# Long convolution by a two-stage FFT with soft-MoE slots: z loads of a pair of chunks in 16 KB rows, issued in the step before, with five z store buffers

## The chip, the cores and the metric

The kernel runs on one core of one Trainium2 chip. The metric is the device time of a run in microseconds. Before the change it is 991.8 us in the median of 11 runs (981.59 to 1000.34).

## The reference, cut to what matters

```
x (8, 5696, 128), h (5696, 128):  y = irfft(rfft(x, 2S) * rfft(h, 2S))[:, :S]      # causal long convolution, per channel
t = y.reshape(45568, 128)
logits = t @ phi                         # phi (128, 32): 8 experts x 4 slots
d = softmax of logits over the tokens    # per slot
slot_input = d.T @ t                     # (32, 128)
slot_out[e] = relu(slot_input[e] @ w1[e]) @ w2[e]     # w1 (8, 128, 1024), w2 (8, 1024, 128)
c = softmax of logits over the slots     # per token
out = c @ slot_out                       # (45568, 128)
```

All data is float32.

## The kernel before

The convolution is a transform of length 90 x 64 in two stages and its inverse in two stages, written as matrix products. The filter h is run through the forward part as group 0, and the 8 batches of x follow as groups 1 to 8. Three kinds of work are interleaved in one loop over `t`, a **step**:

- **A** (`load_x`, `fold`, `stage_a`; steps 0 to 71, eight per group). SP loads a chunk of x (`xc`, three buffers, three steps ahead), GpSimd folds it (L193), TensorE multiplies by `s1` (L204), ScalarE evicts to `fst` (L206, three buffers), and SP stores it to the DRAM tensor `f` (L210, four transfers per step).
- **B** (`load_g`, `stage_b1`, `stage_b2`; from step 9). A group has 23 units, three per step and two in the eighth step. A unit loads `gt` from `f` (L223, five buffers, ordered four units ahead), is transformed (L237, to the PSUM tile `bt`), multiplied by the filter on VectorE (L258, L261, L263), transformed back (L277, to `bz`), evicted by ScalarE to `zst` (L281, **three buffers**) and stored by SP to the DRAM tensor `z` (L282).
- **C** (from step 26). Two chunks are a **pair** T; four pairs (NQ) make a batch. A pair's z (two chunks, two loads of 90 rows x 8 KB, L307) comes into the tiles `zc`. `stage_c1` is the last stage of the inverse transform: four products (L329) of two chunks each, with an eviction to `y` by ScalarE (L338), sums on VectorE (L334, L335) and GpSimd (L348). `stage_c2` to `stage_c6` transpose, form logits and both softmaxes, and add to the slots (L357, L366, L395, L418, L442, L466). A pair takes two steps: c1 is in the even one, c2 and c3 in the odd one.

The order of instructions on each engine is the order in which the program writes them (`tc.manual_schedule()`). Almost all transfers go through SP's queue in that order. They take eight semaphores in rotation, so that a transfer waits for the one that SP issued eight places before, and everything behind it on SP waits too. The banks of PSUM go round in a ring of four; the fourth product of c1 uses the bank that the first one left, so it waits for the eviction by L338.

In a step, the body of the loop has this order: tables, **`load_pair`** (before the change), `load_x`, `stage_a(t, 0)`, dispatch, `slot_b()`, `stage_c1` with `stage_c4` between its products, c2, c6, `slot_b()`, the GpSimd part of c1, c5, `stage_a(t, 1)`, c3, `slot_b()`. A `slot_b()` issues the `gt` load of a unit four ahead, the first half of one unit and the second half (with the z store) of the one before it. The load of a pair is issued at the start of the odd step ahead of its c1:

```
        if pair(1 - 2 * ahead) is not None:
            load_pair(pair(1 - 2 * ahead))
```

`pair(lag)` gives T where the step is `26 + lag + 2 T`. `ahead` is 1 until the last B unit is done (step 81); then memory is free, further z tiles (`zd`) are added to the ring `zring`, and loads are issued a pair earlier. The first load of a batch reads what the last B units of that batch stored, so it has to wait for those stores.

A z load has 90 rows, in partitions 20 to 109 (`Z0 = 20`); a row is 8 KB long in `z`, and rows follow at 64 KB there. The table `i1`, by which c1 multiplies, has its rows in the same partitions, and zeros in the others; the zc tiles are zeroed once in full (L296).

Of the kernel before, what the change touches and what calls it, by code (L numbers as in the profile page):

```python
# [10 lines left out]
F32 = mybir.dt.float32  # L11
# [3 lines left out]
PSUM = bass.MemoryType.PSUM  # L15


def transform_tables(S, N1, N2, CH, Z0, X0, F0, F1):

    N, R1, HALF, P = N1 * N2, S // N2, N2 // 2, 2 * N2
    k1 = np.arange(N1)
    alpha = np.pi * (k1 + 0.5) / N1
    m1 = np.arange(R1) - (N1 - 1) / 2
    a1 = np.outer(m1, alpha)
    s1 = np.stack([np.cos(a1), -np.sin(a1), -np.cos(a1)], 1)
    a0 = np.outer(alpha, np.arange(N1 // 2) + 0.5)
    i1 = np.stack([np.cos(a0), -np.sin(a0), -np.cos(a0)], 1)
    NP = N1 // 2
    part = s1  # L40
    s1 = np.zeros((P, 3, P))
    for a, p in enumerate((F0, F1)):
        s1[X0:X0 + R1, :, p:p + NP] = part[:, :, a * NP:(a + 1) * NP]
    i1 = np.pad(i1[np.arange(N1).reshape(2, N1 // 2).T.reshape(-1)],
                [(Z0, P - N1 - Z0), (0, 0), (0, N2 - N1 // 2)])
    k2 = np.arange(N2)
    omega = np.pi * (k1[:, None] + 2 * N1 * k2[None] + 0.5) / N
    m2 = np.arange(HALF) - (N2 - 1) / 2
    a2 = m2[None, :, None] * omega[:, None, :]
    w = np.concatenate([np.cos(a2), np.sin(a2)], 1)  # L50
    back = np.arange(N2).reshape(2, HALF // CH, CH).transpose(1, 0, 2).reshape(-1)
    NU = (NP + 1) // 2
    turn = (N1 - 1) / 2 * alpha[:, None] + (N2 - 1) / 2 * omega
    wq = np.zeros((2, N2, NP, N2))
    vq = np.zeros((2, N2, NU, 2, N2))
    tn = np.zeros((2, N2, 2, NU, 2))
    for a in range(2):
        wq[a] = w[a * NP:(a + 1) * NP].transpose(1, 0, 2)
        for q in range(NP):
            vq[q % 2, :, q // 2, a] = w[a * NP + q][back].T  # L60
            tn[q % 2, :, 0, q // 2, a] = np.cos(turn[a * NP + q]) / N
            tn[q % 2, :, 1, q // 2, a] = np.sin(turn[a * NP + q]) / N
    wq, vq, tn = [t.reshape(P, *t.shape[2:]) for t in (wq, vq, tn)]
    return [np.ascontiguousarray(t, dtype=np.float32) for t in (s1, i1, wq, vq, tn)]
# [3 lines left out]
def kernel(  # L68
# [24 lines left out]
    nc = tc.nc  # L93
    P = 128
# [14 lines left out]
    NQ = NJ // 2  # L109
    assert S == R1 * N2 and R1 == N1 - 1 and D == P and CH == Q == 4  # L110
    SPLIT = R1 // 16 * 16
    Z0, X0, F0, F1 = 20, 20, 6, 82
    ctx.enter_context(tc.manual_schedule())

    t_s1, t_i1, t_w, t_v, t_turn = [
        nc.inline_tensor(t, f"tab_{n}").ap()
        for n, t in zip(("s1", "i1", "w", "v", "turn"), transform_tables(S, N1, N2, CH, Z0, X0, F0, F1))]
    fd = [nc.dram_tensor(f"f_{g}", (2, N2, NP, 2, D), F32, kind="Internal").ap() for g in range(B + 1)]
    zd = [nc.dram_tensor(f"z_{b}", (NP, 2 * N2, 2, D), F32, kind="Internal").ap() for b in range(B)]
    cd = nc.dram_tensor("c_t", (P, B * NQ, Q, 2, MH), F32, kind="Internal").ap()  # L120
# [50 lines left out]
    def load_x(c):  # L171
        if c >= (B + 1) * NJ:
            return
        g, j = divmod(c, NJ)
        src = (h if g == 0 else x[g - 1]).rearrange("(a n) d -> a n d", n=N2)
        t_ = xcs[c % len(xcs)]
        gap = N2 - CH * (2 * j + 1)
        for r in (slice(0, SPLIT), slice(SPLIT, R1)):
            v = src[r, CH * j:CH * (j + 1), :]
            v = bass.AP(tensor=v.tensor, offset=v.offset,  # L180
                        ap=[v.ap[0], [gap * D, 2], [1, CH * D]])
            nc.sync.dma_start(
                out=t_[X0 + r.start:X0 + r.stop, :, :, :].rearrange("p s n d -> p s (n d)"), in_=v)
        xs[c] = t_
# [82 lines left out]
    def stage_b2(u):  # L267
        g, i = divmod(u, NU)
        if g == 0:
            return  # L270
        n = min(2, NP - 2 * i)
        y_ = prods.pop(u)
        bz = bps.tile([P, 2, 512], F32, name="bz", tag="bz")
        for q in range(n):
            r = slice(q * HP, (q + 1) * HP)
            for a in range(2):
                nc.tensor.matmul(bz[a * HP:(a + 1) * HP, q, 0:2 * D], vt[r, i, a, :],  # L277
                                 y_[r, a, :, :].rearrange("p c d -> p (c d)"),
                                 start=True, stop=True)
        st = bpool.tile([P, 2, 2 * D], F32, name="zst", tag="zst", bufs=3)  # L280
        nc.scalar.activation(st[:, 0:n, :], bz[:, 0:n, 0:2 * D], AF.Copy)  # L281
        nc.sync.dma_start(  # L282
            out=zd[g - 1][2 * i:2 * i + n, :, :, :].rearrange("q r c d -> r q (c d)"),
            in_=st[:, 0:n, :])
# [2 lines left out]

    zs, ys, Ls, ds = {}, {}, {}, {}
    ybufs = [ypool.tile([P, Q * CH, D + 1], F32, name=f"y{i}") for i in range(2)]
    zring = [ypool.tile([P, 2, CH, 2, D], F32, name=f"zc{i}") for i in range(2)]  # L290
    lt = ypool.tile([P, CH, 2, HP], F32, name="lt")
    dt = ypool.tile([P, CH, 2, HP], F32, name="dt")
    om, op = [ypool.tile([P, CH, D], F32, name=n) for n in ("om", "op")]
    yt = ypool.tile([D, Q * CH, 2, MH], F32, name="yt")
    for t_ in zring:
        nc.vector.memset(t_[:, :, :, :, :], 0.0)  # L296
    for t_ in (lt, dt):
        nc.vector.memset(t_[:, :, :, :], 0.0)
    for t_ in ybufs:
        nc.vector.memset(t_[:, :, D:D + 1], 1.0)  # L300

    def load_z(c):
        b, j = divmod(c, NJ)
        t_ = zring.pop(0)
        zring.append(t_)
        w_ = 2 * CH * 2 * D
        nc.sync.dma_start(  # L307
            out=t_[Z0:Z0 + N1, :, :, :, :].rearrange("k o n c d -> k (o n c d)"),
            in_=zd[b].rearrange("q (a r) c d -> (q a) (r c d)",
                                a=2)[:, j * w_:(j + 1) * w_])  # L310
        zs[c] = t_

    def load_pair(T):
        if T < NT:
            load_z(2 * T)
            load_z(2 * T + 1)

    def stage_c1(T, between):
        za, zb = zs.pop(2 * T), zs.pop(2 * T + 1)
        y_ = ybufs[T % 2]  # L320

        def part(v, f):
            k = (2 * v + f) * CH
            return y_[:, k:k + CH, 0:D] if f == 0 else y_[:, k + CH - 1:k - 1:-1, 0:D]

        def product(o, tab, q):
            p = bank()
            for h_, t_ in enumerate((za, zb)):
                nc.tensor.matmul(p[h_ * HP:(h_ + 1) * HP, :], i1[:, tab, :], t_[:, o, :, q, :],  # L329
                                 start=True, stop=True)  # L330
            return p[:, :].rearrange("p (n d) -> p n d", d=D)

        def fold_out(even, minus, plus):
            nc.vector.tensor_tensor(out=plus, in0=even, in1=minus, op=AL.add)  # L334
            nc.vector.tensor_tensor(out=minus, in0=even, in1=minus, op=AL.subtract)  # L335

        b_, a_ = product(0, 1, 1), product(0, 0, 0)
        nc.scalar.activation(part(0, 0), b_, AF.Copy)  # L338
        fold_out(a_, part(0, 0), part(1, 0))
        between()  # L340
        b_, a_ = product(1, 1, 0), product(1, 2, 1)
        nc.scalar.activation(om[:, :, :], b_, AF.Copy)

        def after():
            fold_out(a_, om[:, :, :], op[:, :, :])
            for v, o_ in ((1, op), (0, om)):
                for part_, sign in ((part(v, 1), AL.subtract), (part(v, 0), AL.add)):
                    nc.gpsimd.tensor_tensor(out=part_, in0=part(v, 0), in1=o_[:, :, :], op=sign)  # L348

        ys[T] = y_  # L350
        return after
# [193 lines left out]
    for t in range(steps):  # L545
        us = list(units(t))

        def pair(lag):
            T, half = divmod(t - LAG_C - lag, 2)
            return T if half == 0 and 0 <= T < NT else None  # L550
# [18 lines left out]
        for tab, src, first, n, k in ((wt, t_w, LAG_B - 2, NP, 2 * PER),  # L569
                                      (vt, t_v, LAG_B + NJ - 2, NU, PER)):  # L570
            p0 = k * (t - first)
            if 0 <= p0 < n:
                v = slice(p0, min(n, p0 + k))
                nc.sync.dma_start(out=tab[:, v], in_=src[:, v])
        if pair(1 - 2 * ahead) is not None:
            load_pair(pair(1 - 2 * ahead))
        if t < NA:
            load_x(t + 3)
            stage_a(t, 0)
            fold(t + 1, 0)  # L580
        if pair(3) is not None:
# [11 lines left out]
        if pair(5) is not None:  # L593
            stage_c6(pair(5))
        slot_b()
        if after:
            after()
        if U is not None:
# [21 lines left out]
        if t == last_front:  # L620
            front.close()
            rings.append(mid.enter_context(tc.tile_pool(name="ps2", bufs=4, space=PSUM)))
            last = work.enter_context(tc.tile_pool(name="last", bufs=1))
            tail["last"] = last
            tail["cT"] = last.tile([P, B, R1, 2 * NJ], F32, name="cT")
            tail["pool"] = cload.enter_context(tc.tile_pool(name="cload", bufs=3))
            w2s = last.tile([P, E, NFC, D], F32, name="w2s")
            for i in range(2):
                t_ = last.tile([P, 2, CH, 2, D], F32, name=f"zd{i}")
                nc.vector.memset(t_[:, :, :, :, :], 0.0)  # L630
                zring.insert(i, t_)
            assert pair(1) is not None
            load_pair(pair(1) + 2)
            ahead = 2
# [147 lines left out]
```

## Time and profile before

| | |
|---|---|
| median of 11 runs | 991.8 us (981.59 to 1000.34) |
| the profiled execution | 993.06 us, of which the span from first to last instruction is 991.3 us |
| granted TensorE clock, mean | 0.945 |
| TensorE, VectorE, ScalarE, GpSimd busy | 867.8 us (88%), 675.1 (68%), 510.3 (51%), 462.0 (47%) |
| bytes moved by DMA, mean rate | 272.79 MB, 275 GB/s |
| z loads | 64 transfers of 720 KB (60 to zc, 4 to zd) |
| z stores | 184 transfers, 176 of 256 KB and 8 of 128 KB |
| stages | A alone to about 45 us, A and B to about 190, A, B and C to about 740, B and C to about 830, C alone to about 875, then experts and output |

The page gives busy shares of the engines and the DMA queues over 40 slices of the span. A busy share says how full a resource is; which of the full ones makes the others wait is read from the waits (an engine, its line, what released it, and total, number and longest of such waits), from a tile's view (the same for the instructions of that tile) and from the timeline (single instructions with the idle time ahead of them). In the windows view each row is a stretch of the span with the busy time of PE, PEld, DVE, ACT and POOL, the granted clock, the DMA share and GB/s.

### The profile page before, as it was taken

The numbers are of one execution on the slowest core, as the hardware profiler recorded it, in microseconds if no ns is written. First come the engines' busy times: TensorE is split into PE (matmuls) and PEld (weight loads), VectorE is DVE, ScalarE is ACT, GpSimd is POOL, SyncE is SP. The second block draws the span as 40 slices with busy tenths as digits, with TensorE's granted clock in tenths as the row PEclk, the third lists the DMA queues.
The fourth block names the chain that finished last, engine by engine and source line by source line (L and its number), as shares of the span: only waits on it lengthen the run. The fifth ranks groups of instructions, "written<-read, shape, count | busy, mean of one in ns | idle before, by whom it ended". The sixth has DMA issues, their size and how long they took to land.

```text
span 991.3 us, 20314 instructions
## 1 busy us (share of the span) xinstructions
PE 867.8 (88%) x7220; PEld 406.6 (41%) x7220; DVE 675.1 (68%) x1137; ACT 510.3 (51%) x1051; POOL 462.0 (47%) x427
## 2 busy tenths in 40 slices
PE   6777888799999999999999999999998887785893
PEld 2222233234444444444444444434443343333783
DVE  2034477468888788787878788778877996564542
ACT  3557554345565566556555555556554443442442
POOL 5546533245555555455545555545533442785000
PEclk9989899999999999999999999999999998976875
DMA  7998899899999999999999899999987896942598
GB/s 193 270 276 269 254 330 300 253 314 291 279 289 303 287 285 283 296 291 284 281 301 291 264 300 288 285 268 288 316 262 253 276 290 207 271 174 99 212 405 329
DMA packets 177283, 272.79 MB, mean 275 GB/s; under 512 B 15024, under 2 KB 119728, under 8 KB 171423
## 3 DMA queue, kind: packets, MB, share of 16 engines
q1 hardware_dynamic: 176607, 271.13, 88.3%
q8 instruction: 58, 0.95, 0.4%
q10 hardware_dynamic: 576, 0.36, 0.1%
q14 instruction: 42, 0.34, 0.1%
HBM read 143.04 MB, written 128.39 MB: 274 GB/s over the span
## 4 chain that ended last, share of the span: by engine, by line
PE 51%; DMA 24%; DVE 7%; POOL 6%; ACT 4%; issue 4%; SPq 3%; ACTq 0%; DVEq 0%; POOLq 0%
PE bank L204 16%; DMA z<-zst 11%; PE bank L329 9%; PE bt L237 8%; PE bz L277 6%; DMA zc<-z 5%; POOL y L348 5%; DMA out_dram<-o 4%; PE bank L357 3%; PE bank L442 2%; PE bank L366 2%; DMA f<-fst 1%; SPq L210 1%; DMA gt<-f 1%; DVE yf L263 1%
## 5 line engine op out<-in xcount | busy, mean ns | idle before, releaser
L204 PE MATMUL bank<-x,s 128*128 128x512 f32 x576 | 284.9, 622 | 9.6 <-POOL x L193 7.8
L193 POOL TENSOR_TENSOR x<-xc 128x512 f32<-128x512 f32 x144 | 183.8, 1277 | 144.7 <-PE bank L204 116.2
L281 ACT ACTIVATE zst<-bz 128x512 f32<-128x512 f32 (+1 forms) x184 | 108.2, 588 | 236.1 <-PE bz L277 136.7
L206 ACT ACTIVATE fst<-bank 128x512 f32<-128x512 f32 x288 | 168.3, 597 | 84.8 <-PE bank L204 70.2
L258 DVE TENSOR_TENSOR pr<-bt,Hr 128x512 f32<-128x512 f32 (+1 forms) x184 | 126.6, 688 | 84.6 <-PE bt L237 81.4
L237 PE MATMUL bt<-gt,wt 64*64 64x256 f32 x1620 | 139.4, 408 | 40.0 <-DMA gt<-f 11.4
L263 DVE TENSOR_TENSOR yf<-pr,pi 128x512 f32<-128x512 f32 (+1 forms) x184 | 158.3, 860 | 6.4
L329 PE MATMUL bank<-zc,i 128*64 128x512 f32 x480 | 140.1, 626 | 22.4 <-ACT y L338 15.5
L204 PEld LDWEIGHTS bank<-x,s 128*128 128x128 f32 x576 | 100.4, 193 | 132.5 <-issue 91.6
L277 PE MATMUL bz<-yf,vt 64*64 64x256 f32 x1440 | 119.5, 387 | 7.0 <-DVE yf L263 4.4
L261 DVE TENSOR_TENSOR pi<-bt,Hi 128x512 f32<-128x512 f32 (+1 forms) x184 | 125.2, 681 | 0.0
L237 PEld LDWEIGHTS bt<-gt,wt 64*64 64x64 f32 x1620 | 44.7, 133 | 156.0 <-PE bank L204 54.2
L348 POOL TENSOR_TENSOR y<-y,op 128x512 f32<-128x512 f32 x64 | 75.7, 1184 | 59.1 <-DVE op L334 56.6
L403 POOL MEMSET dt<- 64x8 f32 x32 | 3.4, 107 | 180.8 <-ACT dn L406 121.8
L348 POOL TENSOR_TENSOR y<-y,om 128x512 f32<-128x512 f32 x64 | 85.2, 1331 | 2.5
L357 PE MATMUL bank<-ident,y 109*128 109x109 f32 x512 | 62.4, 270 | 12.7 <-POOL y L348 12.6
L277 PEld LDWEIGHTS bz<-yf,vt 64*64 64x64 f32 x1440 | 53.7, 134 | 46.0 <-issue 9.4
L329 PEld LDWEIGHTS bank<-zc,i 128*64 128x64 f32 x480 | 33.7, 138 | 93.2 <-issue 37.5
L359 ACT ACTIVATE yt<-bank 128x360 f32<-128x360 f32 x128 | 53.0, 471 | 30.4 <-PE bank L357 30.4
L248 DVE SCALAR_TENSOR_TENSOR Hr<-bt,turn,ph 128x128 f32<-128x128 f32 (+1 forms) x46 | 16.1, 349 | 74.8 <-ACT ph L246 74.8
L357 PEld LDWEIGHTS bank<-ident,y 109*128 109x128 f32 x512 | 50.4, 145 | 29.3 <-POOL y L348 20.8
L334 DVE TENSOR_TENSOR y<-bank,y 128x512 f32<-128x512 f32 x32 | 22.1, 691 | 51.2 <-ACT y L338 45.8
(95 smaller groups left out, 915.9 us busy)
## 6 DMA issues: line engine op xcount, KB each, us to landing
f<-fst SPq DMA_DIRECT2D x288, 180.0 KB
gt<-f SPq DMA_DIRECT2D x198, 256.0 KB
z<-zst SPq DMA_DIRECT2D x176, 256.0 KB
zc<-z SPq DMA_DIRECT2D x60, 720.0 KB
xc<-in_x_dram SPq DMA_DIRECT2D x64, 320.0 KB
out_dram<-o SPq DMA_DIRECT2D x16, 1024.0 KB
out_dram<-o SPq DMA_DIRECT2D x8, 768.0 KB
c_t<-cst SPq DMA_DIRECT2D x26, 180.0 KB
```

The source lines that it names most:

```text
L193: nc.gpsimd.tensor_tensor(out=y_[:, :, :], in0=t_[:, 0, :, :], in1=t_[:, 1, ::-1, :], op=AL.subtract if comp else AL.add)
L204: nc.tensor.matmul(p[:, :], s1[:, tab[G], :], src[:, :, :].rearrange("p n d -> p (n d)"), start=True, stop=True)
L206: nc.scalar.activation(st[:, :, G, :], p[:, :].rearrange("p (n d) -> p n d", d=D), AF.Copy)
L237: nc.tensor.matmul(bt[q * HP:(q + 1) * HP, a, 0:2 * D], wt[r, 2 * i + q, :], t_[r, q, :, :].rearrange("p c d -> p (c d)"), start=True, sto ...
L258: nc.vector.tensor_tensor(out=pr[r, :, :, :], in0=pv, in1=Hr[r, i, :, :].unsqueeze(2).broadcast_to([n * HP, 2, 2, D]), op=AL.mult)
L261: nc.vector.tensor_tensor(out=pi[r, :, :, :], in0=pv, in1=Hi[r, i, :, :, :], op=AL.mult)
L263: nc.vector.tensor_tensor(out=y_[r, :, :, :], in0=pr[r, :, :, :], in1=pi[r, :, ::-1, :], op=AL.add)
L277: nc.tensor.matmul(bz[a * HP:(a + 1) * HP, q, 0:2 * D], vt[r, i, a, :], y_[r, a, :, :].rearrange("p c d -> p (c d)"), start=True, stop=True)
L281: nc.scalar.activation(st[:, 0:n, :], bz[:, 0:n, 0:2 * D], AF.Copy)
L329: nc.tensor.matmul(p[h_ * HP:(h_ + 1) * HP, :], i1[:, tab, :], t_[:, o, :, q, :], start=True, stop=True)
L348: nc.gpsimd.tensor_tensor(out=part_, in0=part(v, 0), in1=o_[:, :, :], op=sign)
L357: nc.tensor.transpose(p[:, i * TR:(i + 1) * TR], ys[T][0:TR, k * CH + i, 0:D], ident[0:TR, 0:TR])
```

## The change

The two z loads of a pair (one per chunk, 90 rows of 8 KB) become two loads that hold both chunks (64 rows and 26 rows, each of 16 KB). The 64 rows go to partitions 32 to 95 and the other 26 to partitions 0 to 25, and the rows of `i1` follow them. The two zc tiles become one tile of the same total size. The load of a pair that isn't the first of its batch is issued in the even step, after the second `slot_b()`, which is the step in which the pair before it is read for the last time. The load of a batch's first pair stays at the start of the odd step, now behind `load_x`. With `ahead` at 2 the same places hold, one pair earlier. The z store tile `zst` has five buffers instead of three.

```diff
...
 PSUM = bass.MemoryType.PSUM
-def transform_tables(S, N1, N2, CH, Z0, X0, F0, F1):
+def z_blocks(n):
+
+    return [(0, 64, 32), (64, n - 64, 0)]
+
+
+def transform_tables(S, N1, N2, CH, X0, F0, F1):
...
     s1 = np.zeros((P, 3, P))
     for a, p in enumerate((F0, F1)):
         s1[X0:X0 + R1, :, p:p + NP] = part[:, :, a * NP:(a + 1) * NP]
-    i1 = np.pad(i1[np.arange(N1).reshape(2, N1 // 2).T.reshape(-1)],
-                [(Z0, P - N1 - Z0), (0, 0), (0, N2 - N1 // 2)])
+    part = i1[np.arange(N1).reshape(2, NP).T.reshape(-1)]
+    i1 = np.zeros((P, 3, N2))
+    for r, n, p in z_blocks(N1):
+        i1[p:p + n, :, 0:NP] = part[r:r + n]
     k2 = np.arange(N2)
     omega = np.pi * (k1[:, None] + 2 * N1 * k2[None] + 0.5) / N
     m2 = np.arange(HALF) - (N2 - 1) / 2
...
     NQ = NJ // 2
     assert S == R1 * N2 and R1 == N1 - 1 and D == P and CH == Q == 4
     SPLIT = R1 // 16 * 16
-    Z0, X0, F0, F1 = 20, 20, 6, 82
+    X0, F0, F1 = 20, 6, 82
     ctx.enter_context(tc.manual_schedule())
     t_s1, t_i1, t_w, t_v, t_turn = [
         nc.inline_tensor(t, f"tab_{n}").ap()
-        for n, t in zip(("s1", "i1", "w", "v", "turn"), transform_tables(S, N1, N2, CH, Z0, X0, F0, F1))]
+        for n, t in zip(("s1", "i1", "w", "v", "turn"), transform_tables(S, N1, N2, CH, X0, F0, F1))]
     fd = [nc.dram_tensor(f"f_{g}", (2, N2, NP, 2, D), F32, kind="Internal").ap() for g in range(B + 1)]
     zd = [nc.dram_tensor(f"z_{b}", (NP, 2 * N2, 2, D), F32, kind="Internal").ap() for b in range(B)]
     cd = nc.dram_tensor("c_t", (P, B * NQ, Q, 2, MH), F32, kind="Internal").ap()
...
                 nc.tensor.matmul(bz[a * HP:(a + 1) * HP, q, 0:2 * D], vt[r, i, a, :],
                                  y_[r, a, :, :].rearrange("p c d -> p (c d)"),
                                  start=True, stop=True)
-        st = bpool.tile([P, 2, 2 * D], F32, name="zst", tag="zst", bufs=3)
+        st = bpool.tile([P, 2, 2 * D], F32, name="zst", tag="zst", bufs=5)
         nc.scalar.activation(st[:, 0:n, :], bz[:, 0:n, 0:2 * D], AF.Copy)
         nc.sync.dma_start(
             out=zd[g - 1][2 * i:2 * i + n, :, :, :].rearrange("q r c d -> r q (c d)"),
...
     zs, ys, Ls, ds = {}, {}, {}, {}
     ybufs = [ypool.tile([P, Q * CH, D + 1], F32, name=f"y{i}") for i in range(2)]
-    zring = [ypool.tile([P, 2, CH, 2, D], F32, name=f"zc{i}") for i in range(2)]
+    zring = [ypool.tile([P, 2, 2, CH, 2, D], F32, name="zc")]
     lt = ypool.tile([P, CH, 2, HP], F32, name="lt")
     dt = ypool.tile([P, CH, 2, HP], F32, name="dt")
     om, op = [ypool.tile([P, CH, D], F32, name=n) for n in ("om", "op")]
     yt = ypool.tile([D, Q * CH, 2, MH], F32, name="yt")
-    for t_ in zring:
-        nc.vector.memset(t_[:, :, :, :, :], 0.0)
+    nc.vector.memset(zring[0][:, :, :, :, :, :], 0.0)
     for t_ in (lt, dt):
         nc.vector.memset(t_[:, :, :, :], 0.0)
     for t_ in ybufs:
         nc.vector.memset(t_[:, :, D:D + 1], 1.0)
-    def load_z(c):
-        b, j = divmod(c, NJ)
+    def load_pair(T):
+        if T >= NT:
+            return
+        b, j = divmod(T, NQ)
         t_ = zring.pop(0)
         zring.append(t_)
-        w_ = 2 * CH * 2 * D
-        nc.sync.dma_start(
-            out=t_[Z0:Z0 + N1, :, :, :, :].rearrange("k o n c d -> k (o n c d)"),
-            in_=zd[b].rearrange("q (a r) c d -> (q a) (r c d)",
-                                a=2)[:, j * w_:(j + 1) * w_])
-        zs[c] = t_
-
-    def load_pair(T):
-        if T < NT:
-            load_z(2 * T)
-            load_z(2 * T + 1)
+        w_ = 2 * 2 * CH * 2 * D
+        for r, n, p in z_blocks(N1):
+            nc.sync.dma_start(
+                out=t_[p:p + n, :, :, :, :, :].rearrange("k h o n c d -> k (h o n c d)"),
+                in_=zd[b].rearrange("q (a r) c d -> (q a) (r c d)",
+                                    a=2)[r:r + n, j * w_:(j + 1) * w_])
+        zs[T] = t_
     def stage_c1(T, between):
-        za, zb = zs.pop(2 * T), zs.pop(2 * T + 1)
+        t_ = zs.pop(T)
         y_ = ybufs[T % 2]
         def part(v, f):
...
         def product(o, tab, q):
             p = bank()
-            for h_, t_ in enumerate((za, zb)):
-                nc.tensor.matmul(p[h_ * HP:(h_ + 1) * HP, :], i1[:, tab, :], t_[:, o, :, q, :],
-                                 start=True, stop=True)
+            for h_ in range(2):
+                nc.tensor.matmul(p[h_ * HP:(h_ + 1) * HP, :], i1[:, tab, :],
+                                 t_[:, h_, o, :, q, :], start=True, stop=True)
             return p[:, :].rearrange("p (n d) -> p n d", d=D)
         def fold_out(even, minus, plus):
...
             if 0 <= p0 < n:
                 v = slice(p0, min(n, p0 + k))
                 nc.sync.dma_start(out=tab[:, v], in_=src[:, v])
-        if pair(1 - 2 * ahead) is not None:
-            load_pair(pair(1 - 2 * ahead))
         if t < NA:
             load_x(t + 3)
+        V = pair(1 - 2 * ahead)
+        if V is not None and not V % NQ:
+            load_pair(V)
+        if t < NA:
             stage_a(t, 0)
             fold(t + 1, 0)
         if pair(3) is not None:
...
         if pair(5) is not None:
             stage_c6(pair(5))
         slot_b()
+        V = pair(-2 * ahead)
+        if V is not None and V % NQ:
+            load_pair(V)
         if after:
             after()
         if U is not None:
...
             tail["cT"] = last.tile([P, B, R1, 2 * NJ], F32, name="cT")
             tail["pool"] = cload.enter_context(tc.tile_pool(name="cload", bufs=3))
             w2s = last.tile([P, E, NFC, D], F32, name="w2s")
-            for i in range(2):
-                t_ = last.tile([P, 2, CH, 2, D], F32, name=f"zd{i}")
-                nc.vector.memset(t_[:, :, :, :, :], 0.0)
-                zring.insert(i, t_)
+            t_ = last.tile([P, 2, 2, CH, 2, D], F32, name="zd")
+            nc.vector.memset(t_[:, :, :, :, :, :], 0.0)
+            zring.insert(0, t_)
             assert pair(1) is not None
             load_pair(pair(1) + 2)
             ahead = 2
```

## The prediction

> **What bounds the kernel now.** I read the slices of the page first, then the windows around one z load, then the waits of ScalarE and of the SP queue, then the tile view of zc, and last the timeline of one pair. The page's slices (PE, DMA and GB/s; one slice is 24.8 us):
>
> ```profile
> PE   6777888799999999999999999999998887785893
> ...
> DMA  7998899899999999999999899999987896942598
> GB/s 193 270 276 269 254 330 300 253 314 291 279 289 303 287 285 283 296 291 284 281 301 291 264 300 288 285 268 288 316 262 253 276 290 207 271 174 99 212 405 329
> ```
>
> From about 190 to 740 us two resources are full at once: TensorE at 9, the DMA engines at 9. The rate is only 260 to 300 GB/s, though the end of the kernel reaches 405. The windows show why (us; busy time of PE, PEld, DVE, ACT, POOL; clock, DMA share, GB/s):
>
> ```profile
> 533.00:541.00 8.00, 8.00 (x92) 3.95 (x88) 7.83 (x15) 4.88 (x9) 5.47 (x5) 1.00 1.01 334
> 542.00:550.00 8.00, 8.00 (x66) 3.71 (x68) 6.16 (x9) 5.32 (x12) 4.94 (x5) 1.00 0.93 231
> ...
> 565.00:567.00 2.00, 1.85 (x24) 0.90 (x22) 1.86 (x3) 1.20 (x4) 2.00 (x2) 1.00 0.05 17
> ```
>
> The first window holds small stores and loads, 334 GB/s. The second holds one pair's z load, 231 GB/s with the engines as busy: the z load is the slow transfer. In the packet records its 5760 packets of 8 KB last 502 ns in the mean, the shortest 309; 15 engines at 8 KB per 502 ns are 245 GB/s. The third is a hole in the DMA work at a batch boundary. The waits (total us, times, longest), ScalarE first, then SP:
>
> ```profile
> ACT zst L281 <- DMA z<-zst: 93.5, 28, 5.5
> ```
>
> ```profile
> SPq L282 <- DMA zc<-z: 41.8, 14, 4.2
> ...
> SPq L223 <- DMA zc<-z: 35.0, 17, 3.5
> ...
> SPq L307 <- DMA z<-zst: 23.8, 12, 4.4
> ```
>
> ScalarE stands until an old z store has landed and frees one of three buffers; SP stands behind z loads that have not landed, since an SP transfer waits for the one eight places before it (the instruction list names eight semaphores in rotation). What this does to TensorE is in the tile view of zc (idle ahead of the zc matmuls and weight loads, us, times), and in the timeline of one pair (start, length, what, [idle before it <- releaser]):
>
> ```profile
>   ACT y L338: 46.7, 35
> ...
>   DMA zc<-z: 25.8, 29
> ```
>
> ```profile
> 550.82 2.47 PE L329 MATMUL bank<-zc,i 128*64 128x512 f32 x8
> ...
> 554.03 0.60 ACT L281 ACTIVATE zst<-bz 128x512 f32<-128x512 f32 x1 [3.54 <-DMA z<-zst]
> 554.53 0.59 ACT L338 ACTIVATE y<-bank 128x512 f32<-128x512 f32 x1
> ...
> 555.17 1.08 PE L329 MATMUL bank<-zc,i 128*64 128x512 f32 x4 [0.29 <-ACT y L338]
> ```
>
> ScalarE's zst eviction waits 3.54 us for a store, the y eviction behind it is late, and the fourth product of stage c1 waits for the bank that y frees. Taking from the timeline the first zc matmul of each pair, c1 runs 4.4 us undisturbed (from 290.3 and from 362.9) and up to 7.4 (from 336.4 and 407.4); the excess over 4.4 sums to 38 us over pairs 0 to 23. Landing times agree: the pair that starts at 312.6 has its z landed at 312.3, the one at 550.8 at 550.3, the one at 527.0 at 526.6. Pairs 0 to 23 start at 194.1 and 741.2: 547.1/23 = 23.8 us a pair. Undisturbed, one takes 22.3 (from 290.3, six B units) or 21.6 (from 362.9, five); three of the first and one of the second give 22.1, **TensorE's floor**. The DMA share of the pair from 501.5 to 525.3 is 98.3%, so **DMA's floor is about 23.4**. DMA binds, with TensorE 1.3 us behind it.
>
> [...]
>
> **The change, part by part.** The sum is against the profiled execution (span 991.3 + 1.8 around it = 993.1 us); the median of the runs, 991.8, is 1.3 below.
>
> *Five zst buffers.* A store buffer is needed again after five evictions instead of three. Evictions come every 24/5.75 = 4.2 us, so the allowance goes from some 12 to 21 us, against 8.5 to 10.5 us of store time in the chain (8.52 from 545.40, 10.50 from 640.62) plus SP's lag of 1 to 3 us. The 93.5 us ScalarE stall should nearly vanish, and with it the 46.7 us of idle at c1. Cost: two buffers of memory, no instruction.
>
> *Moving the load.* A pair that isn't the first of its batch is issued four SP transfers earlier (two f stores, one gt load, one z store). In the pair shown the store ahead of the new place went out at 535.67 and the load at 539.8: 3.7 us earlier. The zc buffer is free there: c1's matmuls precede the B matmuls whose store SP has already awaited. Landing was at most 1 us from c1's start, so 3.7 us cover the 25.8 us of waits. What is now behind the load: two f stores (three fst buffers, one and a half steps = 18 us), a gt load (ordered four units = 16 us ahead), a z store (21 us with five buffers). Each takes some 8 us in a full ring: cover enough.
>
> *First pair of a batch.* It stays at the step's start, but behind two x loads (0.9 us of issue, and their wait for GpSimd, up to 2.5 us). The instruction list shows that the 64-row block no longer waits for the batch's last z stores; only the 26-row block does. So 71% of the bytes go out while SP waits, and the 2 us hole of the third window closes: 0.5 to 2 us each, at most 12 in all; part of it is DMA time.
>
> *Shape of the transfer.* As many z issues (64), the same bytes, half the packets. An 8 KB packet of 309 ns against a 4 KB one of 159 leaves 9 ns of fixed cost, so longer runs alone save 6 x 9 = 54 ns per pair and engine. [...] Before, 6 rows per engine twice: 12 x 502 = 6.0 us. [...] I take 0.7.
>
> *Sum.* DMA's floor becomes 23.4 - 0.7 - 0.3 (hole) = 22.4, TensorE's 22.1; two nearly equal limits with jitter give a little more than either, 22.9. Over 23 pairs: 23 x 0.9 = 21 us. The tail's pair at 839.0 has a c1 of 8.2 us and its z landing at 840.6: 2 us. Pairs at 763 to 822 take 19.6 with undisturbed c1s: 0. Before 190 us the zst stall is 93.5 - 86.8 = 6.7 us on ScalarE, of which I take 1. Sum -24: 993.1 - 24 = 969, or 968 on the median's scale; I say **970**.
>
> **Rivals.** *DMA stays at its rate* [...]. Then only jitter and the hole go: 0.4 to 0.6 us of 23.8 per pair, 23 x 0.5 = 12 us: 977 to 986. For it: the slow packets are spread about 500 ns rather than split into 309 and 618. [...]
> *The stall moves* and nothing is won: SP waits for the same landings eight places on, and ScalarE waits for fst buffers or DVE for gt instead. For it: 41.8 + 35.0 us of SP behind zc. Against: those have 16 to 18 us of cover. 987 to 996.
> *Slower*: the 26-row block. [...] the early load stands ahead of f stores and the last z store. At half of 231 GB/s, 426 KB take 3.7 us, and 1049 KB at 231 take 4.5: 8.2 us against 6.4, +1.8 of DMA time per pair. It decides from about +0.4 per pair, where DMA's floor passes 23.8; at +0.9 it is 24.3, 23 x 0.5 = 12 us lost: 1004, at +1.8 about 1024.
> *Not as described*: the second block might wait longer than the whole load did. At batch starts alone, 8 x 1 us; within the stall case.
>
> **How the numbers follow.** Forecast (both floors drop) 0.48, 952 to 980. Rate unchanged 0.24. Stall moves 0.10. Slower 0.18. A measurement of this kernel can tell about 0.5% (5 us) from no change. The first two give faster 0.71, the third same 0.11, the last slower 0.18. Full removal of the 38 us, with the 3 of tail and start and some of the hole, is the low end, 950; the range reaches over the third case to 995.
>
> **What would show it.** Right: ScalarE's wait on z<-zst under 15 us; idle ahead of zc matmuls by y and by zc both under 10; c1 of 4.4 to 5 us; 23 us between pairs; z packets of 16 KB under 900 ns in the mean (two 8 KB ones are 1004); DMA share lower at the same bytes; no hole at batch starts. Wrong: packets near 1000 ns or more, pairs still at 23.5 or above, or a new wait of the same size on fst, gt or x.

## The result and the profile after

The changed kernel takes 975.1 us in the median of 12 runs (969.28 to 984.37), against 991.7 before: ratio 0.984, 95% interval 0.981 to 0.986. The forecast was 970, in a range of 950 to 995. Some runs fall in a slower state (two of these 12 did), and every ratio here compares fast runs with fast runs of the kernel before that were taken beside them, so it is not quite the quotient of the medians. The profiled execution is 971.9 us with a span of 970.1, so 21.1 less than the profiled one of before; the medians differ by 16.6.

In the two profiles, by the first zc matmul of pairs 0, 23 and 31: the start to pair 0 takes 191.3 us (194.1 before), pairs 0 to 23 take 530.7 (547.1), pairs 23 to 31 take 142.3 (143.0), the rest 105.8 (107.1). Of 21.2 us of span, 16.4 come from the stage in which A, B and C overlap. Slices of the page:

```profile
PE   6777788799989998999899989999998886775893
...
DMA  7998899999989998998999899989987884842698
GB/s 197 277 271 273 265 326 337 300 302 300 323 249 307 314 289 244 312 316 260 296 294 288 273 311 313 296 274 351 284 271 256 296 307 151 278 165 113 232 405 329
```

TensorE is as full as before, but every fourth slice or so has an 8, and DMA has 8s beside it: single dips in a faster run. The two waits that the forecast removed are gone from the ordinary pairs. In the tile view of z, what ScalarE's zst eviction waits for z transfers (us, times):

```profile
  ACT zst L288: 3.8, 3
```

It was 95.0 us in the same view before (93.5 of it for z stores). In the tile view of zc, idle time ahead of its matmuls and weight loads, the wait for y is not listed any more (46.7 before), and what is left on z loads are few, long waits:

```profile
  DMA zc<-z: 18.7, 6
  DMA f<-fst: 10.7, 4
```

In the timeline, a c1 of an ordinary pair runs without a gap, 4.4 us from 402.60 to 406.99:

```profile
402.60 1.94 PE L333 MATMUL bank<-zc,i 128*64 128x512 f32 x8
404.47 0.66 PE L399 MATMUL bank<-ident,lt 128*128 128x128 f32 x4
405.05 1.94 PE L333 MATMUL bank<-zc,i 128*64 128x512 f32 x8
```

The six long waits are at batch starts: ahead of the c1 of pairs 0, 4, 12, 16, 20 and 28. That of pair 8 has a wait of 4.40 us as well, put down to `f<-fst`. The timeline of TensorE at pair 4:

```profile
279.22 0.61 PE L284 MATMUL bz<-yf,vt 64*64 64x256 f32 x8
283.40 3.21 PE L333 MATMUL bank<-zc,i 128*64 128x512 f32 x8 [3.57 <-DMA zc<-z]
```

SP's timeline ahead of it shows why the load is late:

```profile
267.43 0.55 SPq L289 DMA_DIRECT2D z<-zst  x1
271.97 0.73 SPq L189 DMA_DIRECT2D xc<-in_x_dram  x2
272.79 1.10 SPq L316 DMA_DIRECT2D zc<-z  x2
```

After the z store of 267.43 SP stands 4 us ahead of the x load. That load overwrites a buffer which GpSimd still has to fold, and GpSimd comes to this fold only behind the sums of the pair before:

```profile
268.25 2.46 POOL L352 TENSOR_TENSOR y<-y,om 128x512 f32<-128x512 f32 x2
270.67 1.27 POOL L200 TENSOR_TENSOR x<-xc 128x512 f32<-128x512 f32 x1
```

Windows over these microseconds (columns as before, DMA share and GB/s last) show the engines run dry:

```profile
268.00:270.00 2.00, 2.00 (x42) 1.12 (x42) 0.90 (x4) 0.73 (x2) 1.92 (x3) 1.00 0.76 232
270.00:272.00 2.00, 2.00 (x24) 1.86 (x28) 1.92 (x3) 1.46 (x4) 2.00 (x3) 1.00 0.00 2
272.00:274.00 2.00, 2.00 (x18) 0.83 (x19) 1.80 (x4) 1.10 (x3) 2.00 (x2) 1.00 0.40 101
```

In SP's waits as a whole this line more than doubled (total, times, longest; first before, then after):

```profile
SPq L182 <- POOL x L193: 30.1, 22, 2.6
```

```profile
SPq L189 <- POOL x L200: 68.2, 29, 4.4
```

So the change took the stalls out of the ordinary pairs, and put a new one at each batch start.

### The profile page after: what moved, and what is told of

The parts are those of the page before. It is cut to its first block, busy times and chain, and to the rows that moved or that the text cites. A ratio compares the mean times of both kernels' runs of the same rounds, so it can differ in the third digit from the quotient of the medians.

```text
span 970.1 us, 20410 instructions
## 1 busy us (share of the span) xinstructions
PE 844.7 (87%) x7220; PEld 404.1 (42%) x7220; DVE 668.2 (69%) x1135; ACT 515.1 (53%) x1051; POOL 462.3 (48%) x427
## 4 chain that ended last, share of the span: by engine, by line
PE 67%; DMA 17%; POOL 6%; DVE 3%; issue 3%; ACT 1%; SPq 1%; DVEq 0%; POOLq 0%; ACTq 0%
PE bank L211 22%; PE bank L333 12%; PE bt L244 11%; PE bz L284 8%; DMA zc<-z 6%; PE bank L361 4%; DMA out_dram<-o 4%; POOL y L352 4%; DMA gt<-f 3%; PE bank L446 3%; PE bank L399 2%; PE bank L370 2%; PE bank L422 1%; PE bank L470 1%; DMA f<-fst 1%
## 5 line engine op out<-in xcount | busy, mean ns | idle before, releaser
L270 DVE TENSOR_TENSOR yf<-pr,pi 128x512 f32<-128x512 f32 (+1 forms) x184 | 153.2, 833 | 6.4
L333 PE MATMUL bank<-zc,i 128*64 128x512 f32 x480 | 124.5, 642 | 23.1 <-DMA zc<-z 18.7
L333 PEld LDWEIGHTS bank<-zc,i 128*64 128x64 f32 x480 | 31.6, 143 | 79.1 <-issue 71.6
L743 PE MATMUL op<-so,cT 32*128 32x128 f32 x704 | 46.4, 376 | 4.5 <-ACT o L752 4.0
```

Of the source, the lines that this page charges most:

```text
L270: nc.vector.tensor_tensor(out=y_[r, :, :, :], in0=pr[r, :, :, :], in1=pi[r, :, ::-1, :], op=AL.add)
```

## The experiments

Each of the three edits was also made alone, and the place has two halves (ordinary pairs, and a batch's first pair). The table has the median, the ratio to before with its 95% interval, the mean time between pairs 0 and 23 in the profile, the time that c1 loses (its length over 4.4 us, and TensorE's idle time just ahead of it), summed over the first pairs 4, 8, 12, 16 and 20 and over the other pairs 1 to 23, and the time that a pair's z packets take per DMA engine (packet records, mean over 16).

| kernel | us | ratio | us per pair | first pairs | others | z packets |
|---|---|---|---|---|---|---|
| before | 991.7 | 1 | 23.79 | 2.8 | 32.7 | 5.66 |
| changed | 975.1 | 0.984 (0.981 to 0.986) | 23.07 | 20.7 | 0.0 | 4.87 |
| zst5_only | 985.9 | 0.994 (0.991 to 0.997) | 23.79 | 10.6 | 27.3 | 5.72 |
| early_only | 973.4 | 0.981 (0.977 to 0.986) | 22.99 | 16.0 | 0.0 | 5.51 |
| early_zst5 | 973.3 | 0.982 (0.978 to 0.987) | 22.82 | 16.4 | 0.0 | 5.46 |
| shape_only | 973.1 | 0.982 (0.978 to 0.986) | 23.10 | 0.0 | 20.3 | 4.85 |
| late_place | 974.0 | 0.982 (0.977 to 0.987) | 22.99 | 2.4 | 15.3 | 4.85 |
| zst3 | 976.8 | 0.987 (0.982 to 0.991) | 22.97 | 20.7 | 0.0 | 4.82 |
| z_ahead_of_x | 958.0 | 0.968 (0.963 to 0.972) | 22.38 | 0.2 | 0.0 | 4.80 |
| split_first | 963.2 | 0.972 (0.968 to 0.977) | 22.46 | 6.6 | 0.0 | 4.84 |
| early_z_ahead | 969.3 | 0.980 (0.972 to 0.989) | 22.83 | 3.4 | 1.7 | 5.43 |
| ports_crowded | 994.6 | 1.007 (1.004 to 1.010) | 23.48 | 28.2 | 0.0 | 6.55 |
| pitch_60k | 978.0, one run | | 23.12 | 22.6 | 0.0 | 4.93 |
| z_ahead_zst3 | 953.5 | 0.965 (0.960 to 0.970) | 22.20 | 0.2 | 0.0 | 4.77 |

**zst5_only.**

```diff
-        st = bpool.tile([P, 2, 2 * D], F32, name="zst", tag="zst", bufs=3)
+        st = bpool.tile([P, 2, 2 * D], F32, name="zst", tag="zst", bufs=5)
```

> The kernel before with five zst buffers and nothing else. Theory (two causes stretch c1: a late y eviction behind zst, and a late z landing; each has to go): ScalarE's wait on z<-zst falls from 93.5 us to under 15 and the idle ahead of the zc matmuls by y from 46.7 to under 15, but the idle by DMA zc<-z grows from 25.8, since TensorE is early at a load that is issued no earlier; 984 to 990 us. Rival (the store stall alone was the loss): the full gain, 975. Rival (DMA bound): within 2 us of 991.7.

As expected: the wait for y is not listed any more, and TensorE waits on the z load instead. The idle time in the tile view of zc:

```profile
  DMA zc<-z: 57.5, 47
```

It was 25.8 on zc and 46.7 on y. The pairs come at 23.79 us as before. Buffers by themselves mostly move the wait on; the runs are 0.6% faster.

**early_only** and **early_zst5.** Both start from the kernel before and move the loads to the changed kernel's places; the second has five buffers as well.

```diff
-        if pair(1 - 2 * ahead) is not None:
-            load_pair(pair(1 - 2 * ahead))
...
             load_x(t + 3)
+        V = pair(1 - 2 * ahead)
+        if V is not None and not V % NQ:
+            load_pair(V)
...
         slot_b()
+        V = pair(-2 * ahead)
+        if V is not None and V % NQ:
+            load_pair(V)
         if after:
```

> The kernel before with the two 8 KB z loads of a pair at the new places (even step for all but a batch's first pair; that one behind the x loads) and nothing else; three zst buffers. Theory of two causes: idle by DMA zc<-z falls under 10 us for the pairs that are not first, the idle by y stays at some 45 us: 986 to 992. Rival (late z landing alone was the loss): 975 to 980.

> The kernel before with the new places and five zst buffers, but 90-row loads of 8 KB at the old partitions. Theory that the transfer's shape gives DMA time that TensorE can use: slower than the changed kernel by 4 to 10 us (979 to 985), periods of the pairs that are not first 22.6 to 23.2 us. Rival (TensorE's 22.3 us binds once both stalls are gone; the shape is worth nothing by itself): 974 to 978, periods of 22.3.

Both times, 973.4 and 973.3, lie outside the theory's range and just below the rival's. The place alone, with 8 KB rows and three buffers, reaches the time of all three edits. In the tile view of zc of early_only:

```profile
  DMA zc<-z: 33.5, 23
  ACT y L338: 3.0, 8
```

The wait for y is gone without a new buffer: ScalarE still waits 43.9 us for z stores in total, but not ahead of c1's y. The idle time on zc sits at the batch starts (in the table 16.0 us at the five first pairs and none at the others). Two more buffers change nothing that the runs can tell. With the old transfers the pairs inside a batch (first zc matmul of its second pair to that of its fourth) come 22.25 us apart in early_zst5, as its rival had it.

**shape_only** and **late_place.** Both put the loads of the changed kernel back where they were; the first has three buffers as well.

```diff
+        if pair(1 - 2 * ahead) is not None:
+            load_pair(pair(1 - 2 * ahead))
         if t < NA:
             load_x(t + 3)
-        V = pair(1 - 2 * ahead)
-        if V is not None and not V % NQ:
-            load_pair(V)
-        if t < NA:
             stage_a(t, 0)
...
-        V = pair(-2 * ahead)
-        if V is not None and V % NQ:
-            load_pair(V)
```

> The kernel before with the new shape alone: 64 and 26 rows of 16 KB, at the old place ahead of the x loads, three zst buffers. Theory: packets as in the changed kernel (mean 866 ns against twice 503), 0.8 us less DMA time per pair, z lands some 1 us earlier and the store stall is a little shorter: 982 to 988. Rival (the shape is worth nothing while ScalarE's stall stands): 990 to 993.

> The changed kernel with its z loads back at the start of the odd step, ahead of the x loads, all pairs alike; shape and five buffers stay. If the earlier issue is needed: slower than the changed kernel by 4 to 10 us through z landings at or after c1's start in the pairs that are not first, while the first pairs, no longer behind the x loads, gain up to 3 us each (six to seven of them). If the first pairs' loss behind the x loads outweighs the early issue: as fast as the changed kernel, 972 to 976, or faster.

The shape alone does more than the forecast range had: 973.1, against 982 to 988. In its tile view of zc the order of the two waits is the reverse of early_only's:

```profile
  ACT y L342: 30.8, 31
  DMA zc<-z: 8.7, 9
```

Its first pairs lose nothing, and the instruction list shows why: the 64-row block goes out ahead of the x loads and some 3.6 us ahead of the 26 rows, for which SP waits for the last z stores; its ordinary pairs keep 20.3 us. late_place shows the same trade beside the changed kernel: 18.3 us less at the first pairs, 15.3 us more at the others, and the time stays.

**zst3.** The changed kernel with three buffers (the edit of zst5_only, reversed).

> The changed kernel with three zst buffers. Theory of two causes: ScalarE's wait on z<-zst comes back at 60 to 95 us, c1 is stretched by y again, 982 to 988. Rival (the loads' earlier landing had removed the store stall too): 975 to 978.

The rival held: 976.8, and c1 is as clean as with five. Once the load is early, three store buffers do.

**z_ahead_of_x.**

```diff
+        V = pair(1 - 2 * ahead)
+        if V is not None and not V % NQ:
+            load_pair(V)
         if t < NA:
             load_x(t + 3)
-        V = pair(1 - 2 * ahead)
-        if V is not None and not V % NQ:
-            load_pair(V)
-        if t < NA:
             stage_a(t, 0)
```

> The changed kernel with one edit: a batch's first z load is issued ahead of the step's x loads instead of behind them. Theory (the x load waits for GpSimd's fold, up to 4.4 us, and holds the z load back; the DMA engines run dry meanwhile, share 0.00 at 270 to 272 us): the idle by DMA zc<-z, 18.7 us in 6 waits, falls under 8, and the time to 962 to 970. Rival (SP then waits as long for the batch's last z stores): 973 to 977.

958.0, 17 us below the changed kernel, by this order alone. The tile view of zc:

```profile
  DMA zc<-z: 6.2, 3
```

c1 loses 0.2 us at the first pairs instead of 20.7. This shows the cause of the new stall: the z load's place behind the x loads.

**split_first.** z_ahead_of_x, and the block of 64 rows of a batch's first pair goes out with the ordinary loads, one step earlier (the second argument of `load_pair` names the blocks to load):

```diff
...
         if V is not None and not V % NQ:
-            load_pair(V)
+            load_pair(V, slice(1 if ahead == 1 else 0, 2))
...
-        if V is not None and V % NQ:
-            load_pair(V)
+        if V is not None and (V % NQ or ahead == 1):
+            load_pair(V, slice(0, 2 if V % NQ else 1))
```

> As z_ahead_of_x, and the 64-row block of a batch's first pair is issued in the even step like the others' loads; only the 26 rows that need the last z stores stay at the start of the odd step. Theory: no idle by DMA zc<-z at first pairs but for the very first, 960 to 968, and no later than z_ahead_of_x. Rival (the last z stores queue behind the 1 MB block, land some 3 us later, and the 26 rows with them): equal to z_ahead_of_x or slower by up to 5 us.

The rival came nearer: the median is 5 us above z_ahead_of_x, though the intervals overlap. The last z store of a batch is issued behind the 1 MB block and lands 6.1 to 8.4 us after its issue, 3.0 to 5.4 in z_ahead_of_x, and SP waits for it with the 26 rows (50.1 us in all, 17.1 in z_ahead_of_x):

```profile
SPq L318 <- DMA z<-zst: 50.1, 14, 8.0
```

**early_z_ahead.** The kernel before, with the places of z_ahead_of_x and no other edit.

> The kernel before with only the places of the z loads changed, and the better ones: even step for all but a batch's first pair, and that one ahead of the x loads, as before. 8 KB packets, 90 rows, three zst buffers. Theory (the time of the z landing against c1's start is the whole matter, shape and buffers are spare): 958 to 962, as the kernel with all three edits and this order, which took 958.0. Rival (shape and buffers are needed to reach TensorE's floor at all pairs): 964 to 972.

969.3 is in the rival's range, with runs spread from 959 to 972. c1 is nearly clean, yet pairs come at 22.83 us. With 16 KB blocks and five buffers it was 22.38; the next run says which of these counts.

**z_ahead_zst3.** z_ahead_of_x with three buffers.

> z_ahead_of_x with three zst buffers instead of five. It divides the 11 us between early_z_ahead (969.3: 8 KB rows, three buffers) and z_ahead_of_x (958.0: 16 KB rows in aligned blocks, five buffers). If the blocks are what counts: 957 to 961. If the buffers are: 966 to 970, with ScalarE's wait on z<-zst at 40 to 65 us.

953.5, somewhat below both ranges: the buffers are worth nothing here, and the blocks are worth the whole of the 16 us to early_z_ahead. Per pair that is 22.83 - 22.20 = 0.63 us, and the z packets take 5.43 - 4.77 = 0.66 us less of each engine. A DMA floor of some 22.8 us with the old shape would fit this, but it is not shown: over pairs 0 to 23 the engines' share is 0.97 in early_z_ahead and 0.98 here. What the trace shows is where TensorE waits in early_z_ahead, from pair 0 to pair 23:

```profile
PE bt L237 <- DMA gt<-f: 5.5, 6, 3.1
PE bz L277 <- ACT zst L281: 3.4, 7, 0.6
```

Here the first is not listed and the second is 0.7 us; ScalarE's wait for z stores in the same stretch is 28.7 us instead of 54.6, and c1 loses 0.2 us instead of 5.1. These make some 13 of the 14.6 us between the two. So much of what the blocks give comes through other transfers, whose landings TensorE and ScalarE wait less for. How much of it is packet time, and how much comes from the 64 rows that needn't wait for a batch's last z stores, was not separated.

Four kernels with three buffers form a square, in which each edit can be read twice:

| three zst buffers | rows of 8 KB | blocks of 16 KB |
|---|---|---|
| loads at the old place | 991.7 (before) | 973.1 (shape_only) |
| loads earlier, a batch's first ahead of x | 969.3 (early_z_ahead) | 953.5 (z_ahead_zst3) |

The blocks are worth 19 and 16 us, the places 22 and 20: the two gains nearly add (the ratios 0.982 and 0.980 give 0.963, measured 0.965). With the places of the change as it was made, a batch's first load behind the x loads, blocks and three buffers take 976.8 (zst3), no less than the blocks alone: what the ordinary pairs gain, the first ones lose.

The windows over 190 to 740 us, for the kernel before, the changed one and this one:

```profile
190.00:740.00 550.00, 527.66 (x4360) 237.12 (x4356) 433.14 (x691) 311.49 (x610) 287.91 (x249) 1.00 0.96 288
```

```profile
190.00:740.00 550.00, 528.57 (x4476) 243.47 (x4476) 441.04 (x711) 321.75 (x622) 292.89 (x254) 0.98 0.93 294
```

```profile
190.00:740.00 550.00, 538.83 (x4665) 247.92 (x4664) 460.34 (x744) 328.40 (x643) 301.43 (x262) 1.00 0.96 305
```

The counts are the better measure: 4360, 4476 and 4665 matmul records in the same 550 us, while busy time differs by 2%. So part of the time in which TensorE counts as busy was waiting before. z_ahead_zst3 is faster than both kernels of this study, and TensorE's 22.20 us per pair is near the forecast's floor of 22.1.

**ports_crowded** and **pitch_60k.** Both start from the changed kernel and change only where the bytes of a z load lie. ports_crowded asks whether the partitions of the rows make their packets slow (theory) or not (rival), pitch_60k whether their distance of 64 KB in `z` does (rival) or not (theory). In pitch_60k, `zrows` starts row r at r times 60 KB, so that it reads wrong rows of z and its output is not the reference's:

```diff
-    return [(0, 64, 32), (64, n - 64, 0)]
+    return [(0, 64, 0), (64, n - 64, 64)]
```

```diff
-                in_=zd[b].rearrange("q (a r) c d -> (q a) (r c d)",
-                                    a=2)[r:r + n, j * w_:(j + 1) * w_])
+                in_=zrows(b, r, n, j * w_, w_))
```

> The changed kernel with the 64 rows at partitions 0 to 63 and the 26 at 64 to 89; the DRAM side, the order and the buffers stay. Theory [...]: the first block's packets go from 801 ns in the mean (a quarter of them at 611) to 1150 or more, few at 611; the z load lands 1 to 2 us later, and the time rises by 5 to 15 us through the first pairs. Rival (the DRAM side makes them slow): packets within 5% of before, the time within 3 us of 975.

> The changed kernel with z rows read at a distance of 60 KB instead of 64 KB: it reads wrong rows of z, of the same number and length, so the output is not the reference's; partitions, order and buffers stay. Theory [...]: packets as in the changed kernel, mean 866 ns, first block 801, second 1017. Rival [...]: mean under 720 ns, most at 611.

Rows at 60 KB leave the packets as they were in one run (877 ns in the mean, 866 in the changed kernel): the 64 KB distance is not what makes them slow. Partitions 0 to 63 make the first block's packets last 1167 ns instead of 801, and the time goes to 994.6, slower than before the change and 20 us above the changed kernel, where 5 to 15 was expected. In the tile view of zc the wait at batch starts grows by more than half, from 18.7 us:

```profile
  DMA zc<-z: 30.3, 7
```

The block holds the same 64 rows of `z` in both kernels, and its packets take 1.46 times as long at the other partitions. So the partitions count; why they do, no run or trace shows. The memory ports after which ports_crowded is named were the author's assumption.

## Why the prediction was right or wrong

- **ScalarE's stall** (93.5 us, to nearly vanish): right, it is 3.8 us. The buffers were not needed for what it cost TensorE: early_only and zst3 are clean of the wait for y at c1 with three.
- **The moved load** (3.7 us earlier): right, and under-sized. In the mean over the ordinary pairs it was issued 13.3 us after the preceding c1 had begun, now 7.3; its last bytes land some 5 us ahead of c1, where before they landed about when c1 began.
- **The first pair of a batch**: the step that failed. The change put this load behind the x loads, and the working took their wait at "up to 2.5 us" from a trace in which they stood behind the z load, counted 0.5 to 2 us of gain for each batch and closed the DMA hole. In the changed kernel SP waits at the x loads for GpSimd up to 4.4 us, and the 64-row block, which could have gone out in that time, waits behind them. The hole at 270 to 272 us is deeper than the one shown of before, and five first pairs lose 20.7 us instead of 2.8 (pairs 0 and 28 another 4.3 and 7.0). The working checked what is now late behind the load of an ordinary pair, and not what now stands ahead of a first one.
- **The shape** (0.7 us per pair taken): right in size, 0.8 (5.66 to 4.87), but the way to it was not shown. That engines would slow each other at some partitions and not at others was the author's assumption, and so were the packet times set for the two blocks, 618 ns (twice the shortest packet of before, 309) and twice 618: they take 801 and 1017. That the partitions are a cause is shown (1167 ns in ports_crowded, 801 in the changed kernel); the distance of the rows is shown not to be one (877 ns in pitch_60k, 866). The 15 engines of a 90-row load are a reading of the packet records of before: from 190 to 740 us, 15 packets of 8 KB are in flight for 38% of the time in which any is, more often than any other number. In shape_only the pairs come 0.7 us closer than before, 23.10 for 23.79.
- **The floors.** TensorE's 22.1 fits the 22.20 of z_ahead_zst3. DMA's 23.4 was too high: with the old transfers early_z_ahead and early_zst5 go at 22.8. A share of 98% was read as a floor, but the engines' busy time is no fixed price: with the same transfers it is 22.8 us per pair before (0.96 of 23.79) and 22.1 in early_z_ahead (0.97 of 22.83).
- **The sum**: 21 us for the stage, measured 16.4; tail 2 against 0.7; start 1 against 2.8; 1.3 after the tail, where none was forecast; in the profile 21.1 of 24, in the medians 16.6. That the size came out near is in part luck: a floor that was too high and a stall that was overlooked lie on opposite sides. With a batch's first load ahead of the x loads the same edits take 958.0, 12 us below the forecast.
- **The rivals.** "DMA stays at its rate" fell with the packet times (866 ns for 16 KB, 502 for 8 KB before). "The stall moves" came true at the batch starts alone, and not on fst or gt but behind the x loads; "not as described" had named the batch starts, with 1 us each. "Slower" took half the rate for the 26 rows, which no trace had shown; in the changed kernel their packets take 1017 ns and the others 801. Slower packets came with 64 rows at partitions 0 to 63: ports_crowded adds 1.7 us of DMA time per pair (6.55 for 4.87), as the rival had it (1.8), and ends 20 us above the changed kernel, not 54 above the forecast; a DMA floor that was too high under it would explain this, but no run isolates it.

Left open: shape_only, early_only and the changed kernel end within 2 us of each other, though what they lose at c1 lies in different places. In the table these losses come to 20.3, 16.0 and 20.7 us over the stage, so nearly equal times follow; whether it is chance that the losses are alike was not tested. Whether five buffers cost something beside three (958.0 and 953.5) is not settled either: the intervals overlap.

## What to carry to other kernels

When a load is moved in a queue that issues in order, ask for every kind of iteration what the transfers now ahead of it wait for; here one swap of two lines at the batch start was worth 17 us, as much as all of the change. A resource that is 98% busy is not shown to be a floor, and a wait that vanishes with a buffer may be only a symptom of a transfer that lands late. Try several places in memory for the rows of a load: here the same bytes cost 801 or 1167 ns a packet by their partitions alone.

## What the runs showed of the hardware

A stall of TensorE can cost more than its length. After the 4.4 us idle at the batch start of 378 us the granted clock was half for 4 us and more (clock, DMA share, GB/s last):

```profile
378.00:379.00 1.00, 1.00 (x4) 0.41 (x6) 0.00 (x0) 0.00 (x0) 0.00 (x0) 0.50 0.71 234
379.00:381.00 2.00, 2.00 (x8) 0.40 (x4) 0.00 (x0) 0.60 (x1) 0.00 (x0) 0.50 0.94 297
381.00:383.00 2.00, 2.00 (x8) 1.01 (x8) 1.19 (x2) 0.24 (x1) 0.00 (x0) 0.52 0.87 264
383.00:385.00 2.00, 2.00 (x16) 0.60 (x16) 0.88 (x2) 1.53 (x4) 0.82 (x2) 1.00 0.99 302
```

That c1 then took 6.7 us instead of 4.4, so a stall of 4.4 us cost 4.4 + 2.3 = 6.7. Two other batch starts, with 3.32 and 3.57 us of idle time, were followed by a slow c1 too. In each slow stretch from 190 to 740 us the clock was at 0.50 for 3.4 or 6.8 us. The drop also came after 2.64 us of idle time (c1 at 471.5: 6.0 us), while 2.88 us at 565.3 and 1.73 at 655.6 left c1 at 4.4. So the length of the idle time alone doesn't tell, in this trace, whether the clock drops.
